# GpSimd's two-operand products moved to VectorE and ScalarE in a delta-rule attention with soft-MoE slots

## The chip, the cores and the metric

The kernel runs on one core of one Trainium2 chip. The metric is the device time of one execution in microseconds. The kernel before has a median of 375.31 us over three runs (373.74 to 383.44). All values are fp32. Busy times, waits and timelines come from one profiled execution.

## The reference

Two blocks follow each other. The first is a delta-rule recurrence over 768 positions, for 4 batches of 8 heads with 48 channels:

```
k_n = k / (norm(k) + 1e-6)
for t in range(S):
    y[:, :, t] = q[:, :, t] @ state
    v_old = kt @ state
    state = state + bt * outer(kt, vt - v_old)
```

The second takes the 3072 rows of 384 channels that come of it, computes logits against `phi` (32 slots), forms slot inputs by a softmax over the rows, sends four slots through each of eight experts (384 to 1024 to 384, with a ReLU between) and mixes the slots back by a softmax over the slots.

## The kernel before

The sequence is cut into N = 12 chunks of 64 positions. In a chunk the recurrence becomes matrix algebra: with the Gram matrix G of the chunk's keys, the update needs the inverse of a unit triangular 64x64 matrix for each of 32 heads. A chunk is held as 128 partitions (two halves `e` of 64 positions) by heads. Each 64x64 matrix is cut in 32x32 blocks; the two diagonal blocks are inverted on VectorE, two chunks (a group) at a time, so there are six groups.

**Preparation** (`prep`, L467; `turn`, L407; `gram`, L419). For every chunk, TensorE turns k and q (L413), ScalarE evicts them, and TensorE forms the products (L431) into two PSUM banks. ScalarE evicts the key products with two copies (`evG`) and the query products with one (`evA`, L448). GpSimd multiplies the latter in SBUF with the causal mask (`mskA`, L453). VectorE gathers the right diagonal block with a predicated copy in SBUF (`pick`, L462).

**Inversion** (`invert`, L487). VectorE transposes the diagonal blocks into rows (`spread`, L498), works out norms (L506 to L520, where L519 writes the diagonal and L517 reads beta), and scales the rows (L524: on VectorE for group 0, on GpSimd for the others). GpSimd clears the target (L491). Then come 31 columns with two VectorE instructions each: a product (L536) and a subtraction (L542), of (j+1)(31-j) elements for column j. Two transposes (`backU`, L556; `backT`, L552) bring the inverse back, once as it is and once transposed.

**Join** (`join`, L563). The inverse of the whole 64x64 matrix needs the block between. GpSimd writes two masked copies of the inverse into the Gram buffer (`zm`, L572) and two of the transposed inverse into a buffer of their own (`tw`, L578); each is a product with a mask column broadcast over 256 or 512 elements. TensorE multiplies (L588), ScalarE evicts with a scale (`evJ`), TensorE multiplies again (L600), and VectorE adds the result to the transposed inverse (`addT`, L606).

**Step** (`step`, L613). GpSimd scales v by the norms (`vs`, L621). TensorE multiplies the state (L636), VectorE subtracts (L638), TensorE applies the inverse (L647), ScalarE evicts, TensorE updates the state (L660) and forms the outputs (L679, L688). `turn_y` and `route` (L699 to L783) follow for the slots. Behind the last chunk come the experts (L863 to L899) and the output (L924, L936).

ScalarE's copies all have line 260, that of the helper `copy`.

**What sets the order.** No order is written down. Each piece of work is an `Op` with an engine, a cost in planned microseconds and lists of what it reads and writes. `Plan.schedule` (L97) places them at build time: of an engine's ready pieces it takes the one with the longest path behind it, corrected by a `key` (a smaller key goes first), gives buffers addresses, and emits all instructions sorted by planned start. Each engine then runs its own instructions in that order, and semaphores enforce the dependences that the framework finds between the written and read addresses. The costs are formulas in elements (`t_act`, `t_dv`, `t_dp`, `t_po`), L262 to L268.

The beta values are loaded by 16 small transfers on GpSimd's queue (`load_beta`, L348, key -900), each writing every second of 16 partitions. The clearing of ten ring buffers for k and q (`pad`, L373) has keys from -1500 up. The first two chunks of k are loaded half by SyncE and half by ScalarE (`head`, L384).

Of the kernel before, what the change touches and what calls it, by code (L numbers as in the profile page):

```python
# [196 lines left out]
def kernel(  # L197
# [61 lines left out]
    def copy(o, i, **kw):  # L259
        S_.activation(o, i, ACT.Copy, **kw)  # L260
# [20 lines left out]


# [75 lines left out]
    POOL("beta", 9.0, load_beta, w=[cbb], key=-900)  # L358
# [60 lines left out]
    def gram(n, j, which):  # L419
# [16 lines left out]
        if "g" in which:  # L436
            def evg(i):
                o = A(GG[n // 2])[:, 1024 * (n % 2):1024 * (n % 2) + 1024].rearrange(
                    "p (h i u j t) -> p i j h u t", i=2, u=2, j=2, t=32)[:, i, j]
                copy(o, x4()[:, i, :, 0:C].rearrange("p h (u t) -> p h u t", u=2))  # L440
            for i in H2:
                ACTO("evG%d.%d.%d" % (n, j, i), 256, lambda i=i: evg(i), r=[ps],
                     w=[(GG[n // 2], (n % 2, j, u)) for u in H2])
        if "a" in which:
            def eva():
                o = A(AA[n]).rearrange("p (j h i t) -> p j i h t", j=2, i=2, t=C)[:, j]
                copy(o, x4()[:, :, :, C:2 * C])
            ACTO("evA%d.%d" % (n, j), 512, eva, r=[ps], w=[(AA[n], j)])  # L448

            def msk():  # L450
                o = A(AA[n]).rearrange("p (j x t) -> p j x t", j=2, t=C)[:, j]
                m = A(cmA).rearrange("p (j t) -> p j t", j=2)[:, j]
                G_.tensor_tensor(o, o, m.unsqueeze(1).broadcast_to([P, H, C]), op=ALU.mult)  # L453
            POOL("mskA%d.%d" % (n, j), t_po(512), msk, r=[cmA], w=[(AA[n], j)])

    def pick(n):

        def go(j):
            x = A(GG[n // 2])[:, 1024 * (n % 2):1024 * (n % 2) + 1024].rearrange(
                "p (h u j t) -> p u j h t", u=2, j=2, t=32)  # L460
            m = (M0() if j else M1()).bitcast(U32).unsqueeze(2).broadcast_to([P, H, 32])
            V.copy_predicated(x[:, j, j], m, x[:, 1 - j, j])  # L462
        for j in H2:
            DVE("pick%d.%d" % (n, j), t_dv(256) + 0.1, lambda j=j: go(j),
                r=[cmk, (GG[n // 2], (n % 2, j, 1 - j))], w=[(GG[n // 2], (n % 2, j, j))])

    def prep(n, split):  # L467
# [8 lines left out]
        if split:  # L476
            pick(n)
# [3 lines left out]
        if not split:  # L481
            pick(n)


    ZU, ZT, TW, ZM, nT = {}, {}, {}, {}, {}

    def invert(gs):  # L487
# [59 lines left out]
        for a, g in enumerate(gs):  # L547
            zt = ZT[g] = pl.buf(1024)
            ZU[g] = (lb, 1024 * a)

            def bt(a=a, zt=zt):
                V.transpose(A(zt).rearrange("p (x i) -> p i x", i=32),  # L552
                            A(tt)[:, 1024 * a:1024 * a + 1024].rearrange("p (i k) -> p i k", k=32))
# [5 lines left out]
            DVE("backT%d" % g, 1.9, bt, r=[tt], w=[zt])  # L559
# [3 lines left out]
    def join(n):  # L563
        g, s = divmod(n, 2)
        tw = TW[n] = pl.buf(1024)
        zt, gg = ZT[g], GG[g]
# [3 lines left out]
        def zmask(h):  # L570
            x = A(lb)[:, la + 512 * s:la + 512 * s + 512].rearrange("p (h j t) -> p j h t", j=2, t=32)[:, h]
            G_.tensor_tensor(gx()[:, :, 3 * h], x, mk(h).unsqueeze(2).broadcast_to([P, H, 32]), op=ALU.mult)  # L572
# [3 lines left out]
        def twmask(h):  # L576
            x = A(zt)[:, 512 * s:512 * s + 512].rearrange("p (x t) -> p x t", t=32)
            G_.tensor_tensor(A(tw).rearrange("p (x c t) -> p c x t", c=2, t=32)[:, h], x,  # L578
                             mk(h).unsqueeze(2).broadcast_to([P, 16, 32]), op=ALU.mult)
        for h in H2:  # L580
            POOL("tw%d.%d" % (n, h), t_po(512), lambda h=h: twmask(h), r=[zt, cmk], w=[(tw, h)])
        pj, pt = pl.buf(1, psum=True), pl.buf(1, psum=True)

        def jp():
            for h in range(H):
                for e in H2:
                    a = 1024 * s + P * h
                    mm(two(F1(pj)[ha(e), 32 * h:32 * h + 32], 256, 32), A(gg)[ha(e), a + 32:a + 96],  # L588
                       two(A(gg)[ha(e), a:a + 32], 96, 32))
        PE("j%d" % n, t_pe(16, 900), jp, r=[(gg, (s, x, y)) for x in H2 for y in H2], w=[pj])  # L590
        for h in H2:
            ACTO("evJ%d.%d" % (n, h), 256, lambda h=h: copy(
                gx()[:, :, 1 + h], F1(pj)[:, 256 * h:256 * h + 256].rearrange("p (h t) -> p h t", t=32),
                scale=(NM0() if h else NM1())), r=[pj, cmk], w=[(gg, (s, 0, 1) if h else (s, 1, 0))])

        def tp():
            for h in range(H):
                for e in H2:
                    a = 1024 * s + P * h
                    mm(F1(pt)[ha(e), C * h:C * h + C], A(gg)[ha(e), a + 32:a + 96],  # L600
                       A(tw)[ha(e), P * h + 32:P * h + 96])
        PE("t%d" % n, t_pe(16, 900), tp, r=[(gg, (s, 0, 1)), (gg, (s, 1, 0)), tw], w=[pt])

        def addt():
# [364 lines left out]
```

## Time and profile before

| What | Value |
|---|---|
| median of three runs | 375.31 us |
| span of the profiled execution | 374.3 us |
| busy TensorE (matmul) | 251.8 us |
| busy VectorE | 261.8 us, 612 instructions |
| busy ScalarE | 135.7 us, 311 instructions |
| busy GpSimd | 136.1 us, 150 instructions |
| granted TensorE clock, mean | 0.837 |

The span runs from the first to the last instruction of one profiled execution; its three timed neighbours ran for 373.74, 375.31 and 383.44 us.

In the profile PE is TensorE's matmul, PEld its weight load, DVE VectorE, ACT ScalarE, POOL GpSimd and SP SyncE; a name with a q behind it is that engine's queue. A row of a group names the line, the engine, the operation, what is written and read, the shape (partitions x elements) and the count, then busy time in us and mean ns of one, then the idle time of the engine ahead of these instructions and what ended it. A row of the timeline begins with start and length in us. A row of waits reads "who, for whom: us in total, times, longest us".

### The profile page before, as it was taken

To read this page: it belongs to the slowest core of one execution; us is meant where nothing else is said; L and a number is where in the kernel's file an instruction comes from. 1 tells how busy PE (TensorE), PEld (TensorE's weight loads), DVE (VectorE), ACT (ScalarE), POOL (GpSimd) and SP (SyncE) were. 2 spreads that over 40 slices of the span, in tenths; PEclk is the share of its full clock that TensorE was granted. 3 is DMA by queue.
4 is the path that set the end of the run, shared out by engine and by line. 5 is a ranking of instruction groups with operands and counts; after the bars stand their busy time and mean duration, and the time that the engine had idled before them with its cause. 6 is when DMAs were issued, how large, how long until landed. Compare 5 with 4: busy or idle time off the path is not lost.

```text
span 374.3 us, 12910 instructions
## 1 busy us (share of the span) xinstructions
PE 251.8 (67%) x5560; PEld 209.4 (56%) x5560; DVE 261.8 (70%) x612; ACT 135.7 (36%) x311; POOL 136.1 (36%) x150
## 2 busy tenths in 40 slices
PE   5157640006898985869697888029897988899950
PEld 4056540005797875749586677028787876337640
DVE  2028899999979999999998999999990321310440
ACT  2047740000465553527475353005333453111330
POOL 3776457467085126290228834107260000000000
PEclk9759975555799996999999896758996999699985
DMA  7237676500044424222402002304884799982187
GB/s 136 39 70 138 114 114 121 93 0 2 3 86 89 88 56 74 38 52 46 86 4 46 2 3 47 112 0 95 272 282 140 228 357 413 415 329 114 42 246 219
DMA packets 89671, 45.01 MB, mean 120 GB/s; under 512 B 78224, under 2 KB 84496, under 8 KB 89616
## 3 DMA queue, kind: packets, MB, share of 16 engines
q1 hardware_dynamic: 85328, 42.53, 42.4%
q10 hardware_dynamic: 3776, 1.57, 1.7%
q8 instruction: 43, 0.70, 0.8%
q0 software_dynamic: 512, 0.10, 0.2%
q14 instruction: 12, 0.10, 0.1%
HBM read 39.47 MB, written 4.72 MB: 118 GB/s over the span
## 4 chain that ended last, share of the span: by engine, by line
DVE 43%; PE 34%; ACT 6%; issue 5%; DMA 4%; SPq 3%; POOL 2%; DVEq 0%; ACTq 0%; POOLq 0%
DVE sb L536 14%; DVE sb L542 13%; ACT sb L260 5%; PE pb L647 4%; PE pb L688 4%; PE pb L863 3%; PE pb L679 3%; DVE sb L462 3%; PE pb L899 3%; PE pb L636 3%; DMA sb<-in_q_dram 3%; PE pb L924 2%; POOL sb L357 2%; DVE sb L519 2%; PE pb L600 2%
## 5 line engine op out<-in xcount | busy, mean ns | idle before, releaser
L260 ACT ACTIVATE sb<-pb 128x384 f32<-128x384 f32 (+4 forms) x232 | 108.6, 520 | 129.7 <-PE pb L647 45.3
L542 DVE TENSOR_TENSOR sb<-sb 128x255 f32<-128x255 f32 (+15 forms) x186 | 73.7, 413 | 2.6
L536 DVE TENSOR_TENSOR sb<-sb 128x255 f32<-128x255 f32 (+15 forms) x186 | 73.5, 411 | 2.5
L453 POOL TENSOR_TENSOR sb<-sb 128x512 f32<-128x512 f32 x24 | 31.1, 1309 | 53.7 <-ACT sb L260 53.5
L647 PE MATMUL pb<-sb 64*64 64x48 f32 x768 | 30.2, 239 | 20.9 <-DVE sb L638 16.7
L647 PEld LDWEIGHTS pb<-sb 64*64 64x64 f32 x768 | 28.2, 155 | 23.0 <-DVE sb L638 16.6
L588 PE MATMUL pb<-sb 64*64 64x64 f32 x384 | 15.4, 234 | 36.3 <-POOL sb L572 36.2
L431 PE MATMUL pb<-sb 48*64 48x128 f32 (+1 forms) x896 | 29.7, 278 | 13.0 <-ACT sb L260 12.9
L621 POOL TENSOR_TENSOR sb<-sb 128x384 f32<-128x384 f32 x24 | 30.3, 1283 | 21.1 <-DMA sb<-in_v_dram 10.0
L462 DVE COPY_PREDICATED sb<-sb 128x256 f32<-128x256 uint32 x24 | 18.9, 789 | 25.5 <-ACT sb L260 25.4
L413 PE MATMUL pb<-sb 128*128 128x128 f32 x192 | 28.7, 299 | 10.9 <-DMA sb<-in_k_dram 4.9
L588 PEld LDWEIGHTS pb<-sb 64*64 64x64 f32 x384 | 13.9, 147 | 37.7 <-POOL sb L572 36.7
L431 PEld LDWEIGHTS pb<-sb 48*64 48x64 f32 x896 | 25.3, 150 | 16.5 <-ACT sb L260 14.9
L572 POOL TENSOR_TENSOR sb<-sb 128x256 f32<-128x256 f32 x24 | 15.3, 657 | 49.0 <-DVE sb L556 49.0
L413 PEld LDWEIGHTS pb<-sb 128*128 128x128 f32 x192 | 23.0, 153 | 14.3 <-POOL sb L373 4.2
L688 PE MATMUL pb<-sb 64*64 64x48 f32 x768 | 28.4, 234 | 0.6 <-ACT sb L260 0.5
L679 PE MATMUL pb<-sb 128*64 128x96 f32 x352 | 20.3, 272 | 12.2 <-ACT sb L260 6.0
L688 PEld LDWEIGHTS pb<-sb 64*64 64x64 f32 x768 | 26.8, 149 | 1.2 <-ACT sb L260 0.7
L260 ACT ACTIVATE sb<-pb,sb 128x256 f32<-128x256 f32 x24 | 10.0, 477 | 46.2 <-PE pb L588 46.1
L578 POOL TENSOR_TENSOR sb<-sb 128x512 f32<-128x512 f32 x24 | 25.6, 1086 | 1.0 <-DVE sb L552 0.6
L679 PEld LDWEIGHTS pb<-sb 128*64 128x64 f32 x352 | 17.5, 153 | 14.8 <-ACT sb L260 7.6
L606 DVE TENSOR_TENSOR sb<-sb,pb 128x512 f32<-128x512 f32 x12 | 8.2, 684 | 19.8 <-PE pb L600 19.7
(108 smaller groups left out, 359.4 us busy)
## 6 DMA issues: line engine op xcount, KB each, us to landing
sb<-in_moe_w_dram SPq DMA_DIRECT2D x24, 512.0 KB, 5.5
sb<-in_moe_w_dram SPq DMA_DIRECT2D x16, 768.0 KB, 12.0
sb<-in_q_dram SPq DMA_DIRECT2D x24, 192.0 KB, 4.0
out_dram<-sb SPq DMA_DIRECT2D x18, 192.0 KB, 3.4
sb<-in_v_dram SPq DMA_DIRECT2D x24, 96.0 KB, 3.0
sb<-in_v_dram SPq DMA_DIRECT2D x48, 48.0 KB, 2.5
sb<-in_k_dram SPq DMA_DIRECT2D x22, 96.0 KB, 2.7
sb<-in_k_dram SPq DMA_DIRECT2D x44, 48.0 KB, 2.4
```

What stands on the lines that cost most here:

```text
L260: S_.activation(o, i, ACT.Copy, **kw)
L413: nc.tensor.transpose(F1(ps)[:, P * h:P * h + P], A(src)[:, a:a + P], ident())
L431: mm(A(ps)[ha(e), i, P * h + C * lo:P * h + C * hi], w[:, 0], w[:, lo:hi].rearrange("p k t -> p (k t)"))
L453: G_.tensor_tensor(o, o, m.unsqueeze(1).broadcast_to([P, H, C]), op=ALU.mult)
L462: V.copy_predicated(x[:, j, j], m, x[:, 1 - j, j])
L536: V.tensor_tensor(p(), v4(tt)[:, :, j:j + 1, 0:m].broadcast_to(sh), v4(lb)[:, :, j:j + 1, j + 1:32].rearrange("p a x i -> p a i x").broadc ...
L542: V.tensor_tensor(t, t, p(), op=ALU.subtract)
L588: mm(two(F1(pj)[ha(e), 32 * h:32 * h + 32], 256, 32), A(gg)[ha(e), a + 32:a + 96], two(A(gg)[ha(e), a:a + 32], 96, 32))
L621: G_.tensor_tensor(x, x, A(nb)[:, a:a + 15:2].unsqueeze(2).broadcast_to([P, H, D]), op=ALU.mult)
L647: mm(F1(pU[j])[ha(e), D * x:D * x + D], A(TW[n])[ha(e), a:a + C], A(R)[ha(e), c:c + D])
L679: mm(F1(pY[j])[ha(1 - e), 2 * D * h:2 * D * h + 2 * D], kq5(n)[:, j, h, e, 1], bd()[:, j, h, e], start=h == 0)
L688: mm(F1(pY[j])[ha(1 - e), D * x:D * x + D], A(AA[n])[ha(e), a:a + C], A(U)[ha(e), c:c + D], start=n == 0 and x == 0)
```

## The change

The four products that combine two tensors on GpSimd leave it. `mskA` is now one VectorE product out of PSUM, and `evA` is gone. `vs` is one VectorE product of 768 elements for a chunk instead of two of 384. `scale` is on VectorE for every group. `zm` is gone: `evG` now evicts the block beside the diagonal already masked (a scale per partition on ScalarE), so that L588's weights are masked and its other operand can be the inverse as it is; `pick` reads PSUM. `tw` stays on GpSimd as `tensor_scalar`, one operand and a number per partition, with 256 elements instead of 512; it reads the transposed inverse from the middle of the buffer that `backT` now writes, and a predicated copy out of PSUM (`put`) replaces `addT`'s addition. One buffer of 2048 for a group replaces one of 1024 for a group and one of 1024 for each chunk. The planner's costs for VectorE change, and the beta load's key goes from -900 to -1490.

```
-    t_dv = lambda c: 0.06 + 0.00104 * c
-    t_dp = lambda c: 0.08 + 0.00104 * c
-    t_po = lambda c: 0.18 + 0.0022 * c
-    t_pt = lambda c: 0.18 + 0.0028 * c
+    t_dv = lambda c: 0.075 + 0.00104 * c
+    t_dp = lambda c: 0.075 + 0.00104 * c
...
+    def CMASK(name, f, **kw):
+        def go():
+            o, i, m = f()
+            G_.tensor_scalar(o, i, m, None, op0=ALU.mult)
+        POOL(name, 0.6, go, **kw)
...
-    POOL("beta", 9.0, load_beta, w=[cbb], key=-900)
+    POOL("beta", 9.0, load_beta, w=[cbb], key=-1490)
...
+            def evg(u):
+                kw = {} if u == j else dict(scale=(M0() if u else M1()))
+                copy(gx()[:, u, j], x4()[:, :, :, 32 * u:32 * u + 32], **kw)
...
+            def pck():
+                m = (M0() if j else M1()).bitcast(U32).unsqueeze(2).unsqueeze(3).broadcast_to([P, 2, HQ, 32])
+                V.copy_predicated(gx()[:, j, j], m, x4()[:, :, :, 32 - 32 * j:64 - 32 * j])
+            DVE("pick%d.%d" % (n, j), t_dp(256), pck, r=[ps, cmk], w=[(GG[n // 2], (n % 2, j, j))])
...
-            ACTO("evA%d.%d" % (n, j), 512, eva, r=[ps], w=[(AA[n], j)])
-                G_.tensor_tensor(o, o, m.unsqueeze(1).broadcast_to([P, H, C]), op=ALU.mult)
-            POOL("mskA%d.%d" % (n, j), t_po(512), msk, r=[cmA], w=[(AA[n], j)])
+                V.tensor_tensor(o, x4()[:, :, :, C:2 * C],
+                                m.unsqueeze(1).unsqueeze(1).broadcast_to([P, 2, HQ, C]), op=ALU.mult)
+            DVE("mskA%d.%d" % (n, j), t_dp(512), msk, r=[ps, cmA], w=[(AA[n], j)])
...
-        if gs[0] == 0:
-            DVE("scale" + tag, t_dv(1024 * G), lambda: scale(V), r=[gm], w=[lb])
-        else:
-            POOL("scale" + tag, t_po(1024 * G), lambda: scale(G_), r=[gm], w=[lb])
+        DVE("scale" + tag, t_dv(1024 * G), lambda: scale(V), r=[gm], w=[lb])
...
-            POOL("zm%d.%d" % (n, h), t_po(256), lambda h=h: zmask(h), r=[(lb, la // 1024), cmk], w=[(gg, (s, h, h))])
...
-            POOL("tw%d.%d" % (n, h), t_po(512), lambda h=h: twmask(h), r=[zt, cmk], w=[(tw, h)])
+            CMASK("tw%d.%d" % (n, h), lambda h=h: (tx()[:, :, 3 * h], tx()[:, :, 1 + h], mk(h)),
+                  r=[(tw, (s, 1)), cmk], w=[(tw, (s, 0))])
...
-                    mm(two(F1(pj)[ha(e), 32 * h:32 * h + 32], 256, 32), A(gg)[ha(e), a + 32:a + 96],
-                       two(A(gg)[ha(e), a:a + 32], 96, 32))
+                    b = la + 512 * s + C * h
+                    mm(F1(pj)[ha(e), C * h:C * h + C], A(gg)[ha(e), a + 32:a + 96], A(lb)[ha(e), b:b + C])
...
-            V.tensor_tensor(x, x, F1(pt).rearrange("p (h t) -> p h t", t=C), op=ALU.add)
-        DVE("addT%d" % n, t_dp(512), addt, r=[pt], w=[tw])
+            V.copy_predicated(tx()[:, :, 1:3], A(cmk)[:, 0:2].bitcast(U32).unsqueeze(1).unsqueeze(3).broadcast_to(
+                [P, H, 2, 32]), F1(pt).rearrange("p (h j t) -> p h j t", j=2, t=32))
+        DVE("put%d" % n, t_dp(512), put, r=[pt, cmk], w=[(tw, (s, 1))])
...
-            POOL("vs%d.%d" % (n, j), t_po(384), scv, r=[nb], w=[(vp, 0), (vp, 1), (vp, 3 + j)])
+            V.tensor_tensor(x, x, m.unsqueeze(3).broadcast_to([P, 2, H, D]), op=ALU.mult)
+        DVE("vs%d" % n, t_dv(768), scv, r=[nb], w=[(vp, 0), (vp, 1), (vp, 3), (vp, 4)])
```

More of the change, by code (lines that the diff above doesn't have):

```diff
@@ L436, in gram @@
         if "g" in which:
[L437 to L443, printed above, removed]
+            gx = lambda: A(GG[n // 2])[:, 1024 * (n % 2):1024 * (n % 2) + 1024].rearrange(
+                "p (h i u j t) -> p u j i h t", i=2, u=2, j=2, t=32)
@@ L475, in prep @@
                 gram(n, j, "g")
-        if split:
-            pick(n)
         for j in H2:
@@ L480, in prep @@
             gram(n, j, "a" if split else "ga")
-        if not split:
-            pick(n)
-    ZU, ZT, TW, ZM, nT = {}, {}, {}, {}, {}
+    ZU, TW, nT = {}, {}, {}
     def invert(gs):
@@ L547, in invert, with bt @@
         for a, g in enumerate(gs):
-            zt = ZT[g] = pl.buf(1024)
+            tw = TW[g] = pl.buf(2048)
             ZU[g] = (lb, 1024 * a)
-            def bt(a=a, zt=zt):
-                V.transpose(A(zt).rearrange("p (x i) -> p i x", i=32),
-                            A(tt)[:, 1024 * a:1024 * a + 1024].rearrange("p (i k) -> p i k", k=32))
+            def bt(a=a, tw=tw):
+                x = A(tw)
+                V.transpose(bass.AP(x.tensor, x.offset + 32, [x.ap[0], [1, 32], [P, 16], [32, 2]]),
+                            A(tt)[:, 1024 * a:1024 * a + 1024].rearrange("p (i y j) -> p i y j", y=16, j=2))
             def bu(a=a):
@@ L558, in invert @@
             DVE("backU%d" % g, 1.9, bu, r=[tt], w=[(lb, a)])
-            DVE("backT%d" % g, 1.9, bt, r=[tt], w=[zt])
+            DVE("backT%d" % g, 1.9, bt, r=[tt], w=[(tw, (s, 1)) for s in H2])
             for s in H2:
```

52 lines of the change are left out of this document (16 added, 36 removed).

## The prediction

> **What bounds the kernel now.** First the page's head and its chain of waits, then busy time by stretch.
>
> ```profile
> span 374.3 us, 12910 instructions
> ...
> PE 251.8 (67%) x5560; PEld 209.4 (56%) x5560; DVE 261.8 (70%) x612; ACT 135.7 (36%) x311; POOL 136.1 (36%) x150
> ...
> DVE 43%; PE 34%; ACT 6%; issue 5%; DMA 4%; SPq 3%; POOL 2%; DVEq 0%; ACTq 0%; POOLq 0%
> ```
>
> ```profile
> 0.00:38.00 38.00, 19.05 (x356) 16.09 (x360) 12.66 (x37) 14.72 (x32) 22.80 (x48) 0.82 0.53 96
> 38.00:277.00 239.00, 157.05 (x3809) 137.43 (x3805) 225.97 (x520) 94.96 (x220) 109.06 (x98) 0.83 0.33 70
> 277.00:320.00 43.00, 37.22 (x924) 32.06 (x922) 10.94 (x31) 17.17 (x42) 4.19 (x5) 0.92 0.81 295
> 320.00:375.00 55.00, 38.47 (x483) 23.81 (x477) 12.22 (x27) 8.81 (x19) 0.00 (x0) 0.82 0.65 218
> ```
>
> The columns are the stretch, its length, busy PE, PEld, DVE, ACT, POOL, then granted clock, DMA share and GB/s. There are four stages. To 38 us the kernel loads and prepares. From 38 to 277 us VectorE is busy for 226.0 of 239.0 us: six 32x32 inversions (62 instructions each, L536 and L542) run there, one joined about every 40 us (239.0 / 6), and this stage sets the time. From 277 to 320 us the last recurrence steps run on TensorE (37.2 of 43.0), then come the experts and the output. The question is how much of VectorE's 226.0 us is work.
>
> ```profile
> L542 DVE TENSOR_TENSOR sb<-sb 128x255 f32<-128x255 f32 (+15 forms) x186 | 73.7, 413 | 2.6
> L536 DVE TENSOR_TENSOR sb<-sb 128x255 f32<-128x255 f32 (+15 forms) x186 | 73.5, 411 | 2.5
> ...
> L462 DVE COPY_PREDICATED sb<-sb 128x256 f32<-128x256 uint32 x24 | 18.9, 789 | 25.5 <-ACT sb L260 25.4
> ...
> L519 DVE COPY sb<-sb 128x32 f32<-128x32 f32 x6 | 7.8, 1293 | 0.1
> ...
> L777 DVE TENSOR_SCALAR sb<-sb 128x4 f32<-128x4 f32 x6 | 2.7, 448 | 0.1
> L516 DVE TENSOR_TENSOR sb<-sb 128x32 f32<-128x32 f32 x6 | 2.5, 421 | 0.2
> ...
> L506 DVE TENSOR_SCALAR sb<-sb 128x32 f32<-128x32 f32 x6 | 2.2, 367 | 0.0
> L517 DVE TENSOR_TENSOR sb<-sb 128x32 f32<-128x32 f32 x6 | 2.1, 358 | 0.2
> ```
>
> ```profile
> 37.99 0.18 DVE L519 COPY sb<-sb 128x32 f32<-128x32 f32 x1
> 38.21 0.19 DVE L536 TENSOR_TENSOR sb<-sb 128x31 f32<-128x31 f32 x1
> ...
> 39.69 0.49 DVE L462 COPY_PREDICATED sb<-sb 128x256 f32<-128x256 uint32 x1 [0.24 <-ACT sb L260]
> ...
> 42.34 1.35 DVE L536 TENSOR_TENSOR sb<-sb 128x175 f32<-128x175 f32 x1
> ...
> 45.39 0.36 DVE L536 TENSOR_TENSOR sb<-sb 128x192 f32<-128x192 f32 x1
> ```
>
> The timeline is the ruler: with GpSimd quiet, an SBUF instruction of 31 elements takes 0.19 us, one of 192 takes 0.36, a predicated copy of 256 takes 0.49, a copy of 32 takes 0.18. The group means lie far above it, and 42.34 shows how: 175 elements took 1.35 us. The GpSimd instructions of that time are these.
>
> ```profile
> L453 POOL TENSOR_TENSOR sb<-sb 128x512 f32<-128x512 f32 x24 | 31.1, 1309 | 53.7 <-ACT sb L260 53.5 <-DVE sb L536 0.3
> L621 POOL TENSOR_TENSOR sb<-sb 128x384 f32<-128x384 f32 x24 | 30.3, 1283 | 21.1 <-DMA sb<-in_v_dram 10.0 <-PE pb L636 6.4 <-DVE sb L520 2.3
> L578 POOL TENSOR_TENSOR sb<-sb 128x512 f32<-128x512 f32 x24 | 25.6, 1086 | 1.0 <-DVE sb L552 0.6 <-DVE sb L779 0.3
> L572 POOL TENSOR_TENSOR sb<-sb 128x256 f32<-128x256 f32 x24 | 15.3, 657 | 49.0 <-DVE sb L556 49.0
> L524 POOL TENSOR_TENSOR sb<-sb 128x1024 f32<-128x1024 f32 x5 | 12.3, 2452 | 11.6 <-DVE sb L517 7.5 <-DVE sb L519 4.1
> L373 POOL MEMSET sb<- 128x256 f32 x10 | 2.7, 317 | 0.0
> ```
>
> ```profile
> L606 DVE TENSOR_TENSOR sb<-sb,pb x12: 675/682/691, 94.6 to 306.5; 128x512 f32<-128x512 f32 x12
> L638 DVE TENSOR_TENSOR sb<-sb,pb x22: 535/548/557, 109.9 to 308.6; 128x384 f32<-128x384 f32 x22
> ```
>
> The last two rows (least, median, most ns) are VectorE instructions with one operand in PSUM: all 34 keep their time whatever GpSimd does. So a VectorE instruction that works out of SBUF can lose about a whole GpSimd product to it, and one that reads PSUM loses nothing.
>
> **The change, part by part.** *What VectorE stops losing.* The inversion's length over its 31 columns is the mean of m(32-m), 176 elements; the ruler gives 0.19 + 145 x 0.17/161 = 0.34 us, and I take 0.33 because two interleaved inversions overlap a little. L536 and L542: 372 x (0.412 - 0.33) = 30.5 us. L462: 24 x (0.789 - 0.49) = 7.2. L519: 6 x (1.293 - 0.18) = 6.7. L506, L516, L517, L777: 6 x (1.594 - 4 x 0.19) = 5.0. Together 49.4 us.
>
> Four of the five GpSimd products go. What stays are 24 masks, with one tensor operand of 256 elements instead of two of 512. The trace has no such instruction. By the nearest rows it takes between 0.32 us (the memset of 256, L373) and 0.66 (the two-operand product of 256, L572). What it takes from VectorE lies between nothing and 24 x 0.66 = 15.8 us; I take 5: the five products of 114.6 us together (31.1 + 30.3 + 25.6 + 15.3 + 12.3) cost VectorE 49.4, or 0.43 of their time, and 24 masks half-way between the bounds would be 11.8 us. So 44.4 us leave VectorE, 33.6 to 49.4 at the ends.
>
> The Trainium skill, SBUF — State Buffer, section Who interferes with whom, says that a VectorE instruction with two SBUF inputs contends with a GpSimd instruction that reads SBUF, not with one that only writes, that one SBUF input outside the two-port modes is safe, and that whoever starts first blocks the other for the whole instruction. The PSUM rows agree with it. It speaks against the change in two ways: a one-operand mask still reads SBUF, and the products moved to VectorE out of SBUF become new victims; if each mask cost its full bound the sum would lose 10.8 us of its gain.
>
> *What VectorE takes on.* The causal mask, 512 out of PSUM: the L606 row, 0.68 us; 20 of the 24 fall behind 38 us: 13.6 us (the other four lie in the first stage, where VectorE is busy for 12.7 of 38.0 us). The scaling of v, 12 of 768 in SBUF: the ruler gives 0.36 + 576 x 0.00106 = 0.97 us, 11.6 in all. The scaling of five inversions, 1024: 0.36 + 832 x 0.00106 = 1.24 us, 6.2. The twelve predicated copies from PSUM for L606's additions: 0.49 + 256 x 0.00106 = 0.76 against 0.68, 1.0. The 24 picks now read PSUM: a PSUM row of 384 takes 0.55 and one of 512 takes 0.68, so 256 would take 0.41, no more than from SBUF; nothing. Together 32.4 us; 28 if these run into each other as the interleaved columns do, 36 if predicated copies from PSUM cost half more than from SBUF.
>
> ScalarE loses L448's 24 copies of 512 and gains only a per-partition scale in 24 others of 256; it is busy for 95.0 of 239.0 us in the long stage, and its work shrinks, so this costs nothing even uncovered.
>
> *The join.*
>
> ```profile
> PE pb L588 <- POOL sb L572: 36.2, 2, 34.7
> ```
>
> L588 waited for the zero masks of L572, which are gone: the product starts at the back transpose's end, 1.3 us (two of 0.66) earlier in each group, and L600 no longer waits for L578. Most of the 34.7 us is the first inversion itself. The steps behind it stand in a stage that VectorE sets, so I count nothing, at best 6 x 1.3 = 8 us. What is late next is L606's successor, which waits for the two masks, since it overwrites what they read. Behind it on VectorE stand the next inversion's columns, and L647 on TensorE waits for it; a mask of 0.66 us at most is what that wait can cost, since VectorE, standing, leaves GpSimd its way.
>
> *The start.* The 16 small beta transfers on GpSimd's queue act as a barrier.
>
> ```profile
> 2.26 3.05 DMA sb<-in_k_dram
> ...
> 20.16 1.86 DMA sb<-in_beta_dram
> ```
>
> ```profile
> 3.66 0.62 ACTq L379 DMA_DIRECT2D sb<-in_k_dram  x1
> ...
> 4.32 1.14 ACTq L383 DMA_DIRECT2D sb<-in_k_dram  x2
> ...
> 11.81 8.90 POOL L357 DMA_DIRECT2D sb<-in_beta_dram x16 [7.83 <-DMA sb<-in_q_dram]
> ...
> 22.12 1.92 ACT L260 ACTIVATE sb<-pb 128x256 f32<-128x256 f32 x5 [14.78 <-DMA sb<-in_beta_dram]
> ...
> 27.44 2.02 DVE L498 STREAM_TRANSPOSE sb<-sb 128x1024 f32<-128x1024 f32 x1
> ```
>
> They wait for every load issued before them (7.83 us for q), and ScalarE's next write waits 14.78 us for them, though it goes elsewhere. The key of -1490 is the second pad's, and the longer path (9.0 planned us of issue) puts the load ahead of that pad, so in the planned order only the first k load stands before it: the transfers start at about 5.3 (its landing), issue for 8.9 and are home 1.3 later (20.71 to 22.02 now): 15.5 instead of 22.0. But the second k load, the q loads and nine pads are now behind the barrier: ScalarE issues its half of k in 0.62 + 1.14 = 1.8 us, and the load takes the 3.05 us of the first. At 20.3 us turn, Gram, eviction and pick of this one chunk follow; for the whole of it the kernel now takes 27.44 - 22.12 = 5.3 us, and with chunk 0 done under the load I take 4. The first inversion's transpose starts at 24.3, 3.1 us earlier. The ends are 0 (all loads behind the barrier cost what it saves) and 6.5 (22.0 - 15.5, nothing behind it counts).
>
> *The sum.* 374.3 - 3.1 (start) - 44.4 + 32.4 (VectorE, 38 to 277) - 0 (join and the stages behind) = 359.2 us, from a span of 374.3. The three runs have 373.74 to 383.44 and a median of 375.31, 1.0 above that span; I forecast 360.
>
> **The rivals.** *Deeper* (about 351): masks take nothing (5 us) and each group's join brings half of its 1.3 us (4): 360 - 9. For it: the wait of L588, and POOL idle behind joins. Against: the masks stand where the other inversion runs.
>
> *The masks hold the port at their full bound* (about 371): 359.2 + 10.8, and the 1.0 between span and median. The change then frees VectorE of little more than it loads on it (34 against 32 us). For it: L578's two-operand masks run during the next inversion. Against: a third to a half of every GpSimd product now meets nothing (0.43). The Trainium skill's rule of SBUF — State Buffer, Who interferes with whom, comes to this if every mask starts first.
>
> *The new order eats the gain* (about 370): the planner places everything by its own costs, so work moves between stages, and TensorE still has the same 43 us after the last join. VectorE's 13.0 idle us in the long stage would have to grow to 24. For it: an order fixed beforehand misfits wherever real times differ. Against: what misfitted most, the port, was in no planned cost and now mostly goes.
>
> *Slower, by the Gram's banks* (about 384):
>
> ```profile
> 35.79 1.10 PE L431 MATMUL pb<-sb 48*64 48x128 f32 x32 [0.26 <-ACT sb L260]
> ```
>
> ```profile
> DVE sb L462 <- ACT sb L260: 25.4, 10, 20.3
> ```
>
> ScalarE emptied the Gram's two banks by itself; now VectorE's in-order queue must come by for the pick and the mask, TensorE waits for the banks, and VectorE waits where the Gram (1.10 us) is late. Twenty such meetings at 1.2 us are 24 us, and 360 + 24 = 384. It decides from 0.8 us each, where the gain of 15 is gone, and passes 2% at 1.2. For it: VectorE waited 25.4 us before L462, in ten waits. Against: 20.3 of them are one wait, behind the start's barrier, so the other nine are 0.6 us each and stand in the sum already; and both new readers stand together, so a meeting is waited for once.
>
> **How the numbers follow.** Forecast 0.58, deeper 0.13, masks 0.09, order 0.12, banks 0.08. A measurement here tells about 2%, 7.5 us, from no change, which is from 367.8 to 382.8. Forecast and deeper are faster but for a little; of masks and order a fifth is still below 367.8: faster 0.73, same 0.19, slower 0.08. The range: the low end adds the ends 6.5, 49.4 and 28 (374.3 - 6.5 - 49.4 + 28 = 346.4, 347 on the runs); the high end 0, 33.6 and 32.4 (373.1), which takes in masks and order and leaves out the banks.
>
> **What would show it.** Right: L536 and L542 at a mean near 0.34 us, L519 at 0.2; GpSimd's busy time near 33 us (136.1 - 114.6 + 11.8); VectorE's busy time in all near 252 (261.8 - 44.4 + 24 x 0.68 + 18.8); the causal mask at 0.68 us; beta's transfers starting near 5 us and home by 16; the last join near 262 instead of 277, with the same 97 us behind it. Wrong: VectorE's means unchanged with only masks left on GpSimd; VectorE idle for more than 24 us between first column and last join, waiting for TensorE or for masks; a first transpose later than 27.4; or a tail behind the last join that grows.

## The result and the profile after

The changed kernel takes 379.58 us (median of 17 runs, 377.41 to 383.84), the kernel before 377.36 us (median of 17 runs, 373.74 to 383.44). The ratio is 1.0084, with an interval from 1.0057 to 1.011: slightly slower, within the 2% that were called no change, and 19.6 us above the forecast of 360. A ratio compares undisturbed executions alone, while a median may hold disturbed ones (one execution of the key alone took 1198.54 us). The page of the changed kernel, its head and the groups that answer to the prediction's:

```profile
span 376.5 us, 12832 instructions
...
PE 248.9 (66%) x5560; PEld 210.0 (56%) x5560; DVE 239.2 (64%) x653; ACT 127.0 (34%) x287; POOL 59.8 (16%) x73
...
L284 POOL TENSOR_SCALAR sb<-sb 128x256 f32<-128x256 f32 x24 | 37.4, 1578 | 167.6 <-DVE sb L542 131.8
L531 DVE TENSOR_TENSOR sb<-sb 128x135 f32<-128x135 f32 (+15 forms) x186 | 60.3, 344 | 1.6
L525 DVE TENSOR_TENSOR sb<-sb 128x192 f32<-128x192 f32 (+15 forms) x186 | 59.7, 341 | 1.8
...
L569 PE MATMUL pb<-sb 64*64 64x64 f32 x384 | 15.8, 248 | 42.1 <-DVE sb L459 41.5
...
L453 DVE COPY_PREDICATED sb<-sb,pb 128x256 f32<-128x256 uint32 x24 | 11.4, 476 | 27.8 <-ACT sb L260 27.8
...
L459 DVE TENSOR_TENSOR sb<-pb,sb 128x512 f32<-128x512 f32 x24 | 16.4, 684 | 7.7 <-ACT sb L260 7.5
...
L585 DVE COPY_PREDICATED sb<-sb,pb 128x512 f32<-128x512 uint32 x12 | 9.2, 769 | 18.2 <-PE pb L580 16.8
```

The line numbers have moved: L525 and L531 are the columns' product and subtraction (L536 and L542 before), L459 is the causal mask, L453 the pick, L585 the copies that replaced L606, L569 the join's first product (L588), L627 the first product of a recurrence step (L647), L284 the masked copies left on GpSimd.

VectorE did become faster. The columns fell from 411 and 413 ns to 341 and 344, and VectorE is busy for 239.2 us instead of 261.8, with 34 us of new work in it. The same stretches as before show what became of it:

```profile
0.00:38.00 38.00, 18.86 (x352) 16.36 (x352) 12.72 (x46) 14.54 (x31) 19.55 (x46) 1.00 0.58 100
38.00:277.00 239.00, 154.46 (x3832) 137.84 (x3834) 198.07 (x539) 86.89 (x198) 36.56 (x23) 0.79 0.34 72
277.00:320.00 43.00, 35.41 (x893) 31.14 (x889) 14.95 (x35) 15.16 (x33) 3.66 (x4) 0.90 0.87 313
```

From 38 to 277 us VectorE now stands idle for 239.00 - 198.07 = 41 us, where it stood idle for 13. It works 28 us less there and waits 28 us more, and the last inversion is turned back 12 us later than before (284.44 against 272.48, rows below). The timeline shows where. First the four Grams of the third group (32 matmuls are one Gram), with the one causal mask that stood between them (the idle time in brackets is what TensorE spent waiting for that mask, to get banks), then the gap itself:

```profile
46.51 1.99 PE L435 MATMUL pb<-sb 48*64 48x128 f32 x32 [0.23 <-ACT sb L260]
...
50.32 3.22 PE L435 MATMUL pb<-sb 48*64 48x128 f32 x64
...
66.65 0.67 DVE L459 TENSOR_TENSOR sb<-pb,sb 128x512 f32<-128x512 f32 x1
...
67.47 1.98 PE L435 MATMUL pb<-sb 48*64 48x128 f32 x32 [13.93 <-DVE sb L459]
```

```profile
81.84 2.00 DVE L546 STREAM_TRANSPOSE sb<-sb 128x1024 f32<-128x1024 f32 x1
...
110.23 0.68 DVE L459 TENSOR_TENSOR sb<-pb,sb 128x512 f32<-128x512 f32 x1
...
110.96 4.54 PE L569 MATMUL pb<-sb 64*64 64x64 f32 x96 [41.51 <-DVE sb L459]
...
111.14 0.68 DVE L459 TENSOR_TENSOR sb<-pb,sb 128x512 f32<-128x512 f32 x1
...
112.02 0.68 DVE L459 TENSOR_TENSOR sb<-pb,sb 128x512 f32<-128x512 f32 x1
...
118.14 1.90 PE L627 MATMUL pb<-sb 64*64 64x48 f32 x59
...
284.44 1.97 DVE L546 STREAM_TRANSPOSE sb<-sb 128x1024 f32<-128x1024 f32 x1
```

The first inversion is transposed back at 81.84 to 83.84, so the first join could start then. It starts at 110.96, when the first of three causal masks has run. L569 reads nothing that the mask writes; what it needs is a PSUM bank. Each Gram fills two, and by the kernel's planned order three Grams, all of the third group (both of chunk 4 and one of chunk 5, counted from 0), are in the six banks that the steps' fixed pair leaves. Their keys' products are out, but the query products wait for the mask on VectorE, and the planned order has the masks behind the columns of two inversions. The first step starts at 118.14; it started at 95.3 before. From 85 to 110 us nothing but VectorE and the starved GpSimd works, and after the jam VectorE runs dry (columns as before: PE, PEld, DVE, ACT, POOL, clock, DMA share, GB/s):

```profile
85.00:110.00 25.00, 0.00 (x0) 0.00 (x0) 25.00 (x64) 0.00 (x0) 20.36 (x7) 0.50 0.00 0
...
135.00:160.00 25.00, 22.06 (x573) 19.36 (x564) 10.97 (x18) 14.77 (x32) 0.00 (x0) 0.97 0.45 81
```

That three Grams could be there at all is new too: the third inversion's first transpose (L490) is at 70.88, ahead of the first step; in the kernel before it came after it, as the first of these rows shows (the second is its last inversion, turned back).

```profile
108.00 2.01 DVE L498 STREAM_TRANSPOSE sb<-sb 128x1024 f32<-128x1024 f32 x1
...
272.48 2.12 DVE L556 STREAM_TRANSPOSE sb<-sb 128x1024 f32<-128x1024 f32 x1
```

By the last step the saving on VectorE has made good the 22.8 us that the first step lost, and little more: the last step's first product of the inverse starts at 307.58 us, at 309.04 before. So gain and loss cancel.

### The profile page after: what moved, and what is told of

The parts are those of the page before. It is cut to its first block, busy times and chain, and to the rows that moved or that the text cites. A ratio compares the mean times of both kernels' runs of the same rounds, so it can differ in the third digit from the quotient of the medians.

```text
span 376.5 us, 12832 instructions
## 1 busy us (share of the span) xinstructions
PE 248.9 (66%) x5560; PEld 210.0 (56%) x5560; DVE 239.2 (64%) x653; ACT 127.0 (34%) x287; POOL 59.8 (16%) x73
## 5 line engine op out<-in xcount | busy, mean ns | idle before, releaser
L260 ACT ACTIVATE sb<-pb 128x384 f32<-128x384 f32 (+4 forms) x184 | 91.7, 525 | 135.8 <-PE pb L627 42.6
L284 POOL TENSOR_SCALAR sb<-sb 128x256 f32<-128x256 f32 x24 | 37.4, 1578 | 167.6 <-DVE sb L542 131.8
L531 DVE TENSOR_TENSOR sb<-sb 128x135 f32<-128x135 f32 (+15 forms) x186 | 60.3, 344 | 1.6
L525 DVE TENSOR_TENSOR sb<-sb 128x192 f32<-128x192 f32 (+15 forms) x186 | 59.7, 341 | 1.8
L435 PE MATMUL pb<-sb 48*64 48x128 f32 (+1 forms) x896 | 29.7, 290 | 27.7 <-DVE sb L459 13.9
L569 PE MATMUL pb<-sb 64*64 64x64 f32 x384 | 15.8, 248 | 42.1 <-DVE sb L459 41.5
L260 ACT ACTIVATE sb<-pb,sb 128x256 f32<-128x256 f32 x48 | 21.4, 479 | 55.1 <-DVE sb L531 39.3
L569 PEld LDWEIGHTS pb<-sb 64*64 64x64 f32 x384 | 14.8, 162 | 43.7 <-DVE sb L459 41.9
L627 PE MATMUL pb<-sb 64*64 64x48 f32 x768 | 28.7, 232 | 10.2 <-DVE sb L618 5.0
L627 PEld LDWEIGHTS pb<-sb 64*64 64x64 f32 x768 | 26.9, 147 | 12.6 <-issue 12.5
L668 PE MATMUL pb<-sb 64*64 64x48 f32 x768 | 27.4, 227 | 2.9 <-issue 2.1
L453 DVE COPY_PREDICATED sb<-sb,pb 128x256 f32<-128x256 uint32 x24 | 11.4, 476 | 27.8 <-ACT sb L260 27.8
L616 PE MATMUL pb<-sb 128*64 128x96 f32 x352 | 20.1, 267 | 4.2 <-DVE sb L749 3.9
L659 PE MATMUL pb<-sb 128*64 128x96 f32 x352 | 20.4, 275 | 3.7 <-ACT sb L260 3.7
L616 PEld LDWEIGHTS pb<-sb 128*64 128x64 f32 x352 | 17.3, 151 | 7.5 <-DVE sb L749 4.2
L459 DVE TENSOR_TENSOR sb<-pb,sb 128x512 f32<-128x512 f32 x24 | 16.4, 684 | 7.7 <-ACT sb L260 7.5
L659 PEld LDWEIGHTS pb<-sb 128*64 128x64 f32 x352 | 17.7, 154 | 5.6 <-ACT sb L260 4.8
L585 DVE COPY_PREDICATED sb<-sb,pb 128x512 f32<-128x512 uint32 x12 | 9.2, 769 | 18.2 <-PE pb L580 16.8
```

The costliest lines, as they stand in the source:

```text
L284: G_.tensor_scalar(o, i, m, None, op0=ALU.mult)
L435: mm(A(ps)[ha(e), i, P * h + C * lo:P * h + C * hi], w[:, 0], w[:, lo:hi].rearrange("p k t -> p (k t)"))
L459: V.tensor_tensor(o, x4()[:, :, :, C:2 * C], m.unsqueeze(1).unsqueeze(1).broadcast_to([P, 2, HQ, C]), op=ALU.mult)
L525: V.tensor_tensor(p(), v4(tt)[:, :, j:j + 1, 0:m].broadcast_to(sh), v4(lb)[:, :, j:j + 1, j + 1:32].rearrange("p a x i -> p a i x").broadc ...
L531: V.tensor_tensor(t, t, p(), op=ALU.subtract)
L569: mm(F1(pj)[ha(e), C * h:C * h + C], A(gg)[ha(e), a + 32:a + 96], A(lb)[ha(e), b:b + C])
```

## The experiments

The theory to be tested: the loss is one jam, made by two parts of the change together, the causal mask that empties banks on a busy in-order engine, and the early beta key, which lets a third group be prepared before the first step. Its rivals: the masked copies starve on GpSimd (16.85 us for four of them, below) and hold up the joins; the new costs give a bad order whatever part is taken out; the early key costs time at the start itself.

**The mask ranked first** (the changed kernel, one edit):

```
-            DVE("mskA%d.%d" % (n, j), t_dp(512), msk, r=[ps, cmA], w=[(AA[n], j)])
+            DVE("mskA%d.%d" % (n, j), t_dp(512), msk, r=[ps, cmA], w=[(AA[n], j)], key=-400)
```

> The changed kernel with one edit: the causal mask on VectorE gets a key that puts it ahead of every other piece once it is ready. Nothing else is moved. Theory (held banks): three Gram products wait in all six free PSUM banks for this mask, which the planner puts last because few steps follow it, so the first join cannot start before 111 us; with the mask first, the first join follows the first inversion (about 87 us), the first step's L647 starts near 95 instead of 118.5, VectorE's idle time between 38 and 277 us falls from 41 us to under 20, and the time to 355 to 362 us. Rival (starved masks): GpSimd's copies of the transposed inverse, up to 13.6 us long, hold the steps back; then the time stays at 374 to 380. Rival (more work than it saves): VectorE's work sets the time whatever the order; then also 374 to 380.

Measured: 370.47 us, ratio 0.9852 (0.982 to 0.9883), above the 355 to 362 expected. The jam is gone. In its timeline the join follows the back transpose at once:

```profile
86.93 1.98 DVE L546 STREAM_TRANSPOSE sb<-sb 128x1024 f32<-128x1024 f32 x1
89.06 3.68 PE L569 MATMUL pb<-sb 64*64 64x64 f32 x64 [33.86 <-DVE sb L546]
```

But only half of the loss came back (9 us of some 19), and the execution with a span of 368.8 us still has VectorE idle for 36.8 us from 38 to 277 (202.25 busy), where under 20 was expected. So the banks' hold is there and can be lifted, and lifting it in this way costs something else.

**ScalarE empties the banks** (the changed kernel; the eviction of before put back, the mask then on VectorE in SBUF):

```
+            ACTO("evA%d.%d" % (n, j), 512, eva, r=[ps], w=[(AA[n], j)])
-                V.tensor_tensor(o, x4()[:, :, :, C:2 * C], m.unsqueeze(1)..., op=ALU.mult)
+                V.tensor_tensor(o, o, m.unsqueeze(1).broadcast_to([P, H, C]), op=ALU.mult)
```

> The changed kernel, but ScalarE again empties the query products' banks with its own copy, and VectorE multiplies with the causal mask afterwards, in SBUF. VectorE's amount of work is the same as in the changed kernel; only who frees the banks differs. Theory (held banks): as with the mask put first, the first L647 near 95 and 355 to 362 us. Rival (starved masks): 374 to 380, since GpSimd's copies are untouched and VectorE works even more out of SBUF. Rival (VectorE's work sets the time): 374 to 380.

Measured: 360.9 us, ratio 0.9596 (0.9561 to 0.9631). The third group still goes first (its first transpose is at 66.80), and the first join follows its transpose:

```profile
66.80 1.91 DVE L494 STREAM_TRANSPOSE sb<-sb 128x1024 f32<-128x1024 f32 x1 [0.28 <-ACT sb L260]
...
85.06 2.02 DVE L550 STREAM_TRANSPOSE sb<-sb 128x1024 f32<-128x1024 f32 x1
...
87.23 3.68 PE L573 MATMUL pb<-sb 64*64 64x64 f32 x64 [22.44 <-DVE sb L550]
...
275.57 1.95 DVE L546 STREAM_TRANSPOSE sb<-sb 128x1024 f32<-128x1024 f32 x1
```

With the banks emptied by ScalarE, the rest of the change comes to about the time that was forecast, the early key included, but not in the forecast's way: the last back transpose starts no earlier than before (275.57 against 274.49), and it is the steps beside and behind the inversions that are earlier (the last one's first product of the inverse starts at 291.49, at 309.04 before).

**Beta's load back at its old place** (the changed kernel, key -900 for -1490):

```
-    POOL("beta", 9.0, load_beta, w=[cbb], key=-1490)
+    POOL("beta", 9.0, load_beta, w=[cbb], key=-900)
```

> The changed kernel with only the beta load's key back at -900. In the planned order the three waiting Gram products are then let go at the first inversion's end instead of behind the third one's. Theory (held banks, and the early beta load lets a third group be prepared and fill the banks): the first L647 at 97 to 104 and 358 to 366 us, though the start itself loses what the early load gains (0 to 3 us). Rival (the key only moves the start): 375 to 380.

Measured: 361.11 us, ratio 0.9636 (0.9568 to 0.9704). The mask still holds banks, but now a Gram waits for it, for 32 us, instead of the first join alone:

```profile
74.51 2.00 DVE L546 STREAM_TRANSPOSE sb<-sb 128x1024 f32<-128x1024 f32 x1
...
84.54 1.98 PE L435 MATMUL pb<-sb 48*64 48x128 f32 x32 [32.05 <-DVE sb L459]
...
86.31 2.72 PE L569 MATMUL pb<-sb 64*64 64x64 f32 x64
```

The join stands behind that Gram on TensorE and is about 10 us late (76.5 to 86.31) rather than 27 (83.84 to 110.96). One edit of a load's place, and the order that follows from it, is worth 18.5 us between two kernels of the same instructions (379.58 - 361.11; 17 by the ratios). The new costs are in this kernel too, so the rival that they give a bad order in any case falls.

**The copies on ScalarE** (the changed kernel; the 24 masked copies leave GpSimd):

```
-            CMASK("tw%d.%d" % (n, h), lambda h=h: (tx()[:, :, 3 * h], tx()[:, :, 1 + h], mk(h)),
+            ACTO("tw%d.%d" % (n, h), 256, lambda h=h: copy(tx()[:, :, 3 * h], tx()[:, :, 1 + h], scale=mk(h)),
```

> The changed kernel, but the 24 masked copies of the transposed inverse run on ScalarE (a copy with a scale per partition) instead of GpSimd, which is then left with clearing alone. The planned order of the first three joins is unchanged. Theory (held banks): the first join still waits until about 111 us and the time stays at 373 to 379. Rival (starved masks): without the copies of up to 13.6 us the first step comes early and the time falls to 358 to 366.

Measured: 376.37 us, ratio 0.9975 (0.9932 to 1.0017). GpSimd is out of the inversions, and the jam is as long:

```profile
PE pb L569 <- DVE sb L459: 40.4, 1, 40.4
```

The rival of the starved copies falls as the cause of the jam: without them the changed kernel's 379.58 us become only some 3 us less.

**The mask alone** (the kernel before, with only the causal mask moved to VectorE out of PSUM and `evA` gone):

> The kernel before with one part of the change: the causal mask is a VectorE product out of PSUM and ScalarE's copy is gone; the other GpSimd products and the late beta load stay. By the sums of the prediction VectorE gains 24 x 0.68 = 16 us of work and loses what L453 took from it, about 16 us. In the planned order the first join finds a bank free at the first inversion's end, so the bad trap of the changed kernel should not close: held banks foresee the first L647 near 95 and 370 to 378 us. Rival (a mask that frees the banks on VectorE is bad in any order): the first L647 beyond 105 and over 383 us.

Measured: 371.93 us, ratio 0.9835 (0.9755 to 0.9916). By itself the mask out of PSUM is a gain, of 0.8 to 2.5%: the third group comes at 107.6 us here, after the first step. Taking one of the GpSimd products away lowers the columns' mean too:

```profile
L532 DVE TENSOR_TENSOR sb<-sb 128x135 f32<-128x135 f32 (+15 forms) x186 | 68.3, 383 | 3.9 <-POOL sb L520 1.3
L538 DVE TENSOR_TENSOR sb<-sb 128x135 f32<-128x135 f32 (+15 forms) x186 | 68.2, 382 | 2.6
```

**The key alone** (the kernel before, with only beta's key at -1490), twice:

> The kernel before with only the beta load's key at -1490. The prediction priced this at -3.1 us at the start. The profile of the changed kernel already shows the first inversion's transpose at 28.1 us against 27.4, so the start should give nothing. Theory: the early load swaps the fifth k load and the fourth q load, and a third group is prepared before the first step (its transpose near 70 us instead of 108); with ScalarE emptying the banks this closes no trap, the first L647 stays near 95, and the time lies at 370 to 380. Rival (the early third group alone is what cost the changed kernel its gain): over 385.

> The kernel before with only the beta load's key at -1490, once more, since the profiled execution of the first such run was disturbed. 386 to 391 us. If the third group is what costs, its first transpose stands near 70 us, three inversions share VectorE before the first step, and VectorE stands idle afterwards (over 25 us between 38 and 277) or the products of GpSimd take more from it than 49 us.

Measured: 389.58 us, ratio 1.03 (1.0215 to 1.0385), and 386.1 us, ratio 1.0242 (1.0142 to 1.0343). The key by itself makes the kernel slower by 9 to 11 us, with no mask in PSUM at all. The first run's expectation of 370 to 380 missed, and its rival came: the early third group has a cost of its own, beside the jam. The second run's timeline and its stretch from 135 to 160 us:

```profile
74.82 1.90 DVE L498 STREAM_TRANSPOSE sb<-sb 128x1024 f32<-128x1024 f32 x1
...
94.28 1.96 DVE L556 STREAM_TRANSPOSE sb<-sb 128x1024 f32<-128x1024 f32 x1
...
98.39 2.36 PE L588 MATMUL pb<-sb 64*64 64x64 f32 x32 [42.03 <-POOL sb L572]
```

```profile
135.00:160.00 25.00, 24.35 (x558) 21.03 (x558) 10.93 (x19) 13.78 (x31) 11.76 (x13) 0.93 0.36 66
```

The third inversion starts 33 us earlier than before (74.82 against 108.00), ahead of the first one's end, which comes 11 us later (94.28 against 83.22), and with it the first join (98.39 against 86.59). Later VectorE has too little to do: 10.93 of 25 us.

**The key alone, the third group held back** (the edit of before, and a chunk's preparation is placed only while 10,000 instead of 9,000 columns of SBUF stay free):

```
-    KT = 9000
+    KT = 10000
```

> The kernel before with the beta load's key at -1490 and KT at 10000, so that the third group is held back as in the kernel before. The early load alone measured 389.6 us. Theory (the third group is what costs): 372 to 379, as the kernel before. Rival (the start itself): 384 to 391.

Measured: 377.0 us, ratio 0.998 (0.9933 to 1.0026).

```profile
112.00 1.99 DVE L498 STREAM_TRANSPOSE sb<-sb 128x1024 f32<-128x1024 f32 x1
```

The third transpose is back at 112.00, and the loss of the key is gone, while the start is as early as in the run above (the first transpose is at 27.7 us in both). So it isn't the start that costs. (The larger room without the early key was not run.)

**The changed kernel, the third group held back** (the changed kernel with KT = 11000):

> The changed kernel with one number changed: the room that the planner keeps free before it turns another chunk (KT) is 11000 columns instead of 9000. The beta load stays early and the mask stays on VectorE out of PSUM, but the fifth chunk's query turn, which closes the third group, is put off until the first joins are through. Theory (the early beta load is bad because a third group is prepared before the first step, and its Grams then hold the banks): the first L627 near 90 to 97 and 356 to 364 us, as with the late beta load. Rival (the early load costs by the start itself, whatever follows): 374 to 382.

Measured: 363.86 us (359.07 to 368.51), ratio 0.9563 (0.9463 to 0.9663), which rests on the executions of 359.07 and 361.88 us. The third inversion's first transpose is at 106.90, and the join follows the back transpose:

```profile
74.90 1.95 DVE L546 STREAM_TRANSPOSE sb<-sb 128x1024 f32<-128x1024 f32 x1
...
76.91 3.68 PE L569 MATMUL pb<-sb 64*64 64x64 f32 x64 [28.64 <-DVE sb L546]
```

Mask in PSUM, early key, copies on GpSimd: all of the change stands, without the third group ahead of the first step, and some 19 us come back.

**Both cures at once** (ScalarE empties the banks, and the key is back):

> The changed kernel with both edits that helped singly: ScalarE empties the query products' banks again, with the mask on VectorE in SBUF, and the beta load's key is back at -900. If held banks were the one cause, either edit alone lifts it and the two together add little: 356 to 361 us. If the early third group has a cost of its own (VectorE idle while it waits for the fourth), the two add up: 348 to 355.

Measured: 360.21 us, ratio 0.9546 (0.9483 to 0.961), beside 360.9 and 361.11 for either alone. They don't add up, as two ways to undo one jam shouldn't. The three are not told apart; this one is 4.5% below the kernel before.

**Two operands for the copies** (the kernel above, with `tensor_tensor` and a broadcast mask in place of `tensor_scalar`):

```
-            G_.tensor_scalar(o, i, m, None, op0=ALU.mult)
+            G_.tensor_tensor(o, i, m.unsqueeze(2).broadcast_to([P, H, 32]), op=ALU.mult)
```

> The kernel of the run with both edits, with the 24 masked copies on GpSimd written as a product of two operands, the second a mask column broadcast, over the same 256 elements; everything else and the planned order are the same. The one-operand form took 0.94 us in the changed kernel, the two-operand form 0.62 for 256 elements in the kernel before. If the form sets GpSimd's duration the copies take 0.62 again. The time should be the same within 1% of that run; if the one-operand form spares VectorE its waits, L525 and L531 get longer here.

Measured: 362.33 us, ratio 0.96 (0.9537 to 0.9663): not told apart from the 0.9546 of the kernel above. The groups of the copies, first with one operand, then with two:

```profile
L284 POOL TENSOR_SCALAR sb<-sb 128x256 f32<-128x256 f32 x24 | 26.0, 1103 | 167.6 <-DVE sb L546 125.0 <-DVE sb L715 29.7 <-DVE sb L535 12.8
```

```profile
L284 POOL TENSOR_TENSOR sb<-sb 128x256 f32<-128x256 f32 x24 | 18.7, 809 | 171.9 <-DVE sb L546 140.0 <-DVE sb L715 32.0
```

The form with a number per partition is the slower one on GpSimd, and it spares VectorE next to nothing (the columns' means are 339 ns with it, 342 and 343 without). What helped was that the other products left, not that these have one operand.

**The mask first and the third group held** (the first experiment's edit and KT = 11000):

> Both edits at once: the causal mask ranked ahead of the columns (alone 370.5 us) and the third group held back until the first step is placed (alone 363.9 us). If what was left of the loss with the mask first comes from the third inversion standing ahead of the first step, which leaves VectorE without work around 135 to 160 us (13.3 of 25 us busy there), then the third spread moves to about 100 us, VectorE is busy for over 20 of those 25 us, and the time falls to 360 to 365 us. If ranking the mask first is dear in itself, by breaking into the columns, VectorE is busy there but the time stays near 370 us.

Measured: 375.18 us (371.56 to 378.71), ratio 0.999 (0.9933 to 1.0047). The first reading falls: the third inversion's first transpose is at 109.7 and VectorE is busy for 20.56 of the 25 us from 135 to 160, and still the time is some 14 us above the 359.07 and 361.88 us of the kernel with the group held and the mask not ranked first. So ranking the mask ahead of the columns is dear in itself in this plan. The first back transpose is 4.8 us later (79.7 against 74.9), and step 7's product of the inverse starts at 247.4 against 223.9. These rows show the larger part of it:

```profile
231.40 1.83 PE L616 MATMUL pb<-sb 128*64 128x96 f32 x32
...
246.70 0.55 DVE L618 TENSOR_TENSOR sb<-sb,pb 128x384 f32<-128x384 f32 x1
...
247.39 3.33 PE L627 MATMUL pb<-sb 64*64 64x48 f32 x58 [14.15 <-DVE sb L618]
```

VectorE's subtraction for step 7 (L618, L638 before) starts 13.5 us after the product of the state that it reads (L616) has ended, with the columns of two inversions ahead of it on VectorE. With the group held alone it starts at 219.86, beside its product of 218.93. The first experiment has a wait of the same kind, of 8.66 us. Why the rank leads the planner to this order wasn't settled. The runs also say how far the order alone goes here: kernels with the same instructions lie between 360 and 380 us.

## Why the prediction was wrong, point by point

**VectorE stops losing: right, and too small.** The forecast removed 44.4 us and added 32.4. The columns went to 341 and 344 ns where 0.33 to 0.34 us was forecast; the pick took 476 ns, no more than the 0.49 of its quiet time in SBUF. Added were 16.4 us of masks, 11.7 of scalings of v, 5.1 of scalings of the inversions (7.3 instead of 2.2) and 1.0 of L585, 34.2 in all; VectorE's total fell by 261.8 - 239.2 = 22.6, so 56.8 us left it. The copies on GpSimd cost it about 1.7 us, where 5 were taken (with the copies on ScalarE it is busy for 237.5 us instead of 239.2), and small instructions that the ruler had not listed were freed too. The forecast of its busy time, 252, was 13 us too high.

**The masks' price: wrong way round.** One operand was put between 0.32 and 0.66 us. Alone it takes 0.94, and GpSimd was busy for 59.8 us against a forecast of 33. The sum depended on what this takes from VectorE, and it took little; GpSimd paid instead:

```profile
86.85 16.85 POOL L284 TENSOR_SCALAR sb<-sb 128x256 f32<-128x256 f32 x4 [62.88 <-DVE sb L542]
...
88.28 0.71 DVE L525 TENSOR_TENSOR sb<-sb 128x207 f32<-128x207 f32 x2
```

Four copies took 16.85 us here, the first of them 13.65, with columns of two inversions beside them on VectorE, which kept their time (two instructions of 207 elements in 0.71 us; the ruler gives 0.38 for one). The rule that the prediction took from the Trainium skill, SBUF — State Buffer, section Who interferes with whom, that the one who starts first blocks the other for the whole instruction, is stated there for VectorE's two-port modes; for two SBUF inputs, as here, the section says that the two contend. The trace agrees that these two meet and one is held up; in this stretch that was GpSimd, over many instructions of VectorE and not one.

**The start: one of the two terms that failed.** The prediction priced the early key at -3.1 us, with ends of 0 and -6.5, by looking at the first transpose alone. Its place in the queues was read rightly, but not what it sets free:

```profile
4.88 8.91 POOL L361 DMA_DIRECT2D sb<-in_beta_dram  x16 [3.27 <-DMA sb<-in_k_dram]
...
16.64 0.62 ACTq L383 DMA_DIRECT2D sb<-in_k_dram  x1
17.31 1.40 ACTq L387 DMA_DIRECT2D sb<-in_k_dram  x2
...
22.83 1.94 PE L417 MATMUL pb<-sb 128*128 128x128 f32 x8 [1.43 <-POOL sb L483]
...
28.05 2.01 DVE L490 STREAM_TRANSPOSE sb<-sb 128x1024 f32<-128x1024 f32 x1
```

The transfers started at 4.88 and ScalarE got on at 16.64, near the 15.5 of the forecast; but its half of k, issued until 18.7, was turned at 22.83 instead of 20.3, and the first transpose came at 28.05 instead of 24.3 (before: 27.44). So the start gained nothing. Beyond it the same key let the plan prepare a third group before the first step. That alone costs the kernel before 9 to 11 us, and holding that group back takes the loss away (386.1 and 377.0 us). In the changed kernel it cost 18.5 us. No term of the sum and no end of the range had it.

**Slower, by the Gram's banks: the other term that failed, the right place and the wrong shape.** The sum put the mask's new place at its 13.6 us of work and its wait for banks at nothing. This rival named the cause, VectorE's in-order queue standing between the Gram and its banks, but priced it as twenty meetings of 1.2 us and set it aside because nine of the ten waits before the pick were short. Those were VectorE's waits for ScalarE. Nothing in the trace of before could show how long TensorE would wait for VectorE (the changed kernel's plan could, see below), and the argument that both readers stand together was about the code's lines, not about the order: the pick is wanted by the next inversion and runs early, the mask is wanted by a late step and runs behind two inversions. It was one wait of 41.5 us, which put the first step back by 22.8 (118.1 against 95.3). Together with the key: 361 without the one or the other, 380 with both. The kernel's own plan has this wait: `Plan.schedule` places the first back transpose of the changed kernel at 67.24 planned us, but the first join at 96.23, behind a causal mask at 95.39, and the plan as a whole is 329.1 planned us long, against 313.9 with the key at -900.

**The join** was counted at nothing, which the runs without the jam bear out: it follows the back transpose, and what went to TensorE's wait for L572 was the inversion itself.

**What would show it wrong** was named: idle VectorE over 24 us before the last join (it is 41), and a first transpose later than 27.4 (it is 28.05). Both came.

The 361 us of the kernel with the key undone look like the forecast of 360. Its long stage also ends some 15 us early, as forecast (the last back transpose starts at 258.70 us, at 274.49 before), so the row to set beside the 239.0 us from 38 to 277 is this one:

```profile
38.00:261.00 223.00, 154.00 (x3862) 136.15 (x3862) 204.16 (x559) 89.84 (x203) 28.50 (x25) 0.83 0.37 79
```

The terms differ. VectorE works 204.2 us there, 10 less than the 214.0 that the forecast makes of 226.0, and it idles for 18.8 us instead of 13.0. The first transpose is at 26.71 us, 0.7 earlier than before instead of 3.1, and without the early key. These misses nearly cancel, so that the number came out is in part luck. And where ScalarE empties the banks the same time is reached though the inversions end no earlier than before.

What stays open: why the early third group costs 10 us in the kernel before and nothing in the end once ScalarE empties the banks and GpSimd's products are gone (360.9 and 360.21 with and without it, though the first step is at 96.84 with it and at 85.07 without), and what in the planner makes ranking the mask first dear.

## What to carry to other kernels

When an eviction moves from one engine to another, ask what the new engine's queue holds ahead of it, and who wants the PSUM bank rather than the data: the order ranks by the data, and the bank is not in it. When a load moves, follow what it lets the planner start, not only what it lets arrive. Where a plan is made at build time, read in it when the first join and the first step start, and compare its length between kernels of the same costs (here the kernels at 360 to 361 us have plans of 311 to 316 planned us, those at 370 and 375 of 319 and 320, those at 376 and 380 of 329). Price each part of a change alone and in company; here the mask alone was a gain of 5 us and the key alone a loss of 10, and in the changed kernel the key cost 18.5.

## What the runs showed of the hardware

On GpSimd a product of 256 elements with a number per partition took 0.94 us (median of 24, where nothing stood in its way), the product of 256 with a second tensor 0.62: one operand less was half as slow again. And with instructions of two SBUF operands running back to back on VectorE, a single GpSimd copy took 13.65 us while VectorE's kept their quiet time; before, with larger products on GpSimd, VectorE had lost 49.4 us by the prediction's estimate. What decides which of the two is held up no run here shows. Instructions of VectorE with an operand in PSUM kept their time throughout (684 ns for a product of 512 elements, L606 before and L459 after).
